# A fused long-convolution and MLP block on one core: integer table arguments, a buffer of their own for the small ones, and another order of the operations

## The chip, the cores and the metric

The kernel runs on one core of one Trainium2 chip. The metric is device time in microseconds. The kernel before takes 191.58 us (median of three runs, 191.40 to 192.06).

## What is computed

The input `x` has 2048 rows of 640. It is normalised (`xn`). Branch A makes `kv` from `k` (four taps of a short convolution) times `v`, convolves it causally with a filter of length 2048 per channel, and multiplies by `xn`. Branch B is an MLP with 1728 hidden units. The output joins them:

```python
xn = _layernorm(x)
kv = k_shift * v                        # k_shift: 4 taps, shift_k
y  = irfft(rfft(kv, 2*S) * rfft(ssm_k, 2*S))[:S] + kv * ssm_D
s  = xn * y
g  = silu(gelu(xn @ w1 + b1) @ w2 + b2)
return x + s * g
```

## The kernel before

**The transform by matmuls.** The two Fourier transforms are done in two steps of matmuls each. Step 1 uses a table `W` (128 x 16 x 128, bf16) of sines: for the filter (`K1_0` to `K1_15`, tile by tile, with `K1r_Q` for the last 128 channels of four tiles) and for `kv` (`U1_i`, `U1r_Q`). The casts that evict their PSUM banks are `Ke_i`, `Ker_Q`, `Ue_i`, `Uer_Q` (L175). A staged group of four tiles lies in half of the tile `st` and goes to DRAM in one 1.31 MB write, `Ks_Q` to `scrK` and `Us_Q` to `scrU` (L357). It comes back in another layout by eight loads each, `KL_s` (L528) and `UL_s` (L530), a load waiting for all four writes of its tensor. Step 2 (`K2`, `U2`, L544; `X2`, L559) uses the small table `F2`, followed by casts `Kf`, `Uf`; the products `pr`, `pq` (L571) and the first inverse step `i1`, `i1r` (L587, L615) with the small table `I1`; casts `ie`, `ir`; a write `cs_s` to `scrC` (L627), eight loads `cl_r` (L635), and the last step `i2_i` (L643) with the transposed `W` (`G`, from `gt0`, `gt1`).

**The MLP.** `f1` (L423) multiplies by `w1` in blocks of 128 hidden units, one chunk of 512 rows at a time (chunk 0 is partly cut into halves of 256); `ge` is its gelu on ACT (L427). `f2_i_h` (L463) multiplies tile `i` by half `h` of `w2` in 14 matmuls; `si` (L470) is the SiLU, `gx` (L473) the product with `xn`. A `/N` in the order cuts a matmul into two of 64 columns. `ym`, `ad`, `os` (L647, L651, L653) finish an output tile.

**Other parts.** `bn`, `rs`, `xn` are the layer norm (L370, L384, L391), `xt` and `xe` (L401, L404) the transposes of chunks 0 and 1, `xT2` and `xT3` (L409) those of chunks 2 and 3 by DMA. `kv0` to `kv4` (L502 to L511) are the short convolution on DVE: kv0 to kv2 cover four tiles each and take eight operations of 128 x 2560, kv3 and kv4 two tiles each and 128 x 1280. `U1_i` needs the kv of its tile: `U1_8` to `U1_11` need kv2, `U1_12` and `U1_13` kv3, `U1_14` and `U1_15` kv4. `wu0` to `wu5` (L321) are matmuls on zeros, `xl`, `Kl`, `kl`, `vl`, `w1l`, `w2l`, `skl` the loads of the inputs.

**The tables.** `grid` (L208, POOL) writes two ramps `tq` and `mq`, `fix` (DVE) shifts half of one. For three groups of tiles `wq0`, `wq1`, `wq2` (tiles 0 to 3, 4 to 9, 10 to 15) DVE makes the arguments: the product (L223), the same plus a quarter turn (L225), and an AND of each with 8191 (L226, L227). They lie as int32 in the still empty tile `w2`. `ws0` to `ws2` (L232, ACT) take two sines of each group. The small tables `F2` and `I1` get their arguments from `sm0` (POOL), `sm1` (DVE), `sm2` (POOL) and `sm3` (DVE, AND with 31), in the last quarter of `st`; `ss` (L277, ACT) takes their sines and `sx` (POOL) scales `I1`. The pool of staging slots lets the last quarter of `st` be used for other things only when all these operations are through (L325).

**What sets the order.** The program is a plan: each operation names its engine, what it reads and what it writes. A string `ORDER` lists all operations by hand; they are emitted in that order, so each engine's queue holds its own in that order, DMA queues included (SP for most transfers, POOL for a few). A name may carry the slots it takes (`@2.0`: PSUM banks or staging slots) and its engine (`/A`, `/D`, `/G`, `/S` for ACT, DVE, POOL, SP). Waits come from the buffers alone.

Of the kernel before, what the change touches and what calls it, by code (L numbers as in the profile page):

```python
# [110 lines left out]
def h3_block(ctx: ExitStack, tc: tile.TileContext, x_d, k_d, v_d, sk_d, K_d, D_d, w1_d, b1_d, w2_d, out_d):  # L111
    nc = tc.nc
    sb = ctx.enter_context(tc.tile_pool(name="sb", bufs=1))
# [104 lines left out]
    for g in range(len(TB) - 1):  # L218
        a, b = TB[g], TB[g + 1]

        def wq(e, a=a, b=b):
# [1 line left out]
            nc.vector.tensor_tensor(out=Pm[:, a:b, :], in0=tq[:, a:b, None].to_broadcast([P, n, 64]),  # L223
                                    in1=mq[:, None, :].to_broadcast([P, n, 64]), op=ALU.mult)
            nc.vector.tensor_single_scalar(out=Pc[:, a:b, :], in_=Pm[:, a:b, :], scalar=3 * L // 4, op=ALU.add)  # L225
            nc.vector.tensor_single_scalar(out=Pm[:, a:b, :], in_=Pm[:, a:b, :], scalar=L - 1, op=ALU.bitwise_and)  # L226
# [445 lines left out]
wu4@0 K1_15@2 Ke_15/A sm1 wq0 ws0 xl0 bn0 xl3 bn1 bn5 wu0@1 K1r_3@4 bn4 Ker_3/A id wu5@0 Kl2 sm2 sm3 b1c rs0 bn7 ss
rs1 K1r_1@6.2 gt1@1 K1_7@2 xn0 xn1 skl bn6 wu1@0 xt0@4.0 rs3 Ke_7/A xt1@5 K1_4@2 xe1/D xe0/A xl2 bn3 bn2 Ker_1/A w1l1
K1_6@4 Ke_6/A f1_0_0_2@0.0 xn4 Ke_4/A f1_0_0_4@6 w1l0 kl0 f1_0_0_1@7 xn6 xn5 xn7 f1_0_0_0@4 gte1/A xt4@5.1 xe4/A xt6@2
xt5@3 xe5/A ge_0_0_0 xt7@1 xe6/D f1_0_0_3@2 rs2 xn3 xt3@5 ge_0_0_4 xe7/D ge_0_0_3 f1_1_0_0@1.1 ge_1_0_0 w1l3
# [5 lines left out]
kv2_1a Ke_8/A Ks_2 f1_0_0_5@2 kv2_2m@0 kv2_2a kv2_3m@0 ge_0_0_5 f1_0_0_7@3 ge_0_0_7 U1_2@6.2 U1_3@4 Ue_3/A U1_0@0
Ue_0/A f1_1_0_3@2 kv2_3a kv2_4 ge_1_0_3 Kl1 Ue_2/A f1_1_0_10@3 ge_1_0_10 f1_1_0_4@4 w2l0 ge_1_0_4 f1_0_1_0@5 w2l1
U1r_0@0 Uer_0/A U1_1@6 Ue_1/A Us_0 f1_1_0_7@2 ge_1_0_7 ge_0_1_0 f1_1_0_9@3 ge_1_0_9 f1_0_0_10@4 ge_0_0_10 K1_2@0.0 kl3
kv3_0@0 K1_1@6 K1_3@2 kv3_1m@1 kv3_1a Ke_3/A f1_0_0_9@5 Ke_2/A ge_0_0_9 kv3_2m@1 f1_0_0_11@4 ge_0_0_11 kv3_2a Ke_1/A
Da f1_0_1_4@2 ge_0_1_4 f1_1_0_11@3 ge_1_0_11 K1r_0@0 Ker_0/A K1_0@4 kv3_3m@1 Ke_0/A U1_4@6.2 Ue_4/A f1_0_1_1@2 kv3_3a
# [5 lines left out]
Kf_2_1/A f2_3_0@4.0 Kf_0_0/A f2_3_1 si_3 bn11 bn8 gt0@6 KL3/G@2 K2_3_0@0 gte0/A Kf_3_0/D rs5 xn15 rs4 gx_2 K2_3_1@2  # L691
Kf_3_1/A K2_2_0@4 Kf_2_0/A f2_1_0@6.1 xn12 KL7@5 xn8 K2_7_0@0 Kf_7_0/A xn9 UL0@6 X2_0@2 xn13 xn14 Uf_0_2/D Kf_0_2/D
U2_0_0@4 Uf_0_0/A UL1@3 xn11 f2_1_1 si_1 U2_1_1@0 U2_1_0@4 Uf_1_0/A K2_7_1@2 Kf_7_1/A U2_0_1@6 gx_3 xn10 Uf_1_1/D gx_1
Uf_0_1/A UL2@8 f2_0_0@4.0 U2_2_1@0 Uf_2_1/A pr_1_0@0 X2_1@2 Kf_1_2/A pr_1_1@1 pr_0_0@2 Uf_1_2/A KL4/G@9 K2_4_0@6
Kf_4_0/A pr_0_1@3 f2_0_1 xT3@1 si_0 i1_1@0.2 ie_1_1/D ie_1_0/A X2_2@6 Kf_2_2/D f1_3_0_6@4.1 ge_3_0_6 f1_3_0_3@5
# [60 lines left out]
```

## Time and profile before

| | |
|---|---|
| median of three runs | 191.58 us |
| the profiled execution | 192.54 us |
| its span | 190.8 us |
| mean granted clock of PE | 0.978 |
| busy: DVE / ACT / POOL | 153.9 / 138.7 / 30.0 us |
| HBM read, written | 31.95 MB, 18.35 MB |

The span is the profiled execution from its first to its last instruction; 1.74 us of the 192.54 lie around it. PE is the matrix engine, PEld its loading of weights, DVE, ACT and POOL the vector, scalar and GpSimd engines, SP the one that issues most DMAs; "SPq" is the issue of a DMA by SP's queue. In the lines of the timeline, the first number is the start and the second the duration in microseconds; what stands in brackets is the idle time before an instruction and who ended it. In the rows by window come, behind the window, its length and the busy time of each engine with its number of instructions.

### The profile page before, as it was taken

The page shows a single profiled execution, that of the slowest core. Times are in us where ns is not written, and L with a number is a line of the kernel's source. Part 1 is how long each engine was busy: PE and PEld are TensorE (multiplying, and loading weights), DVE is VectorE, ACT ScalarE, POOL GpSimd, SP SyncE. Part 2 cuts the span into 40 slices and gives each one's busy share as a digit, 9 for nine tenths or more (in the row PEclk, how much of TensorE's full clock was granted, in tenths as well). Part 3 has the DMA queues.
Part 4 walks back from the last instruction along what each step waited for, and adds up shares of the span by engine and source line. Part 5 has one row for each costly group of instructions (what it writes and reads, how often), then busy time and mean ns, then how long its engine had stood idle before and what let it go on. Part 6 is the DMA issues. An engine that isn't in the chain of part 4 may idle for free.

```text
span 190.8 us, 5537 instructions
## 1 busy us (share of the span) xinstructions
PE 176.1 (92%) x2377; PEld 103.8 (54%) x2377; DVE 153.9 (81%) x241; ACT 138.7 (73%) x194; POOL 30.0 (16%) x61
## 2 busy tenths in 40 slices
PE   7889999999889874999979999999999999999991
PEld 2338564443456532566646444545454567679991
DVE  7999999999999891397995869799698511789983
ACT  5999999999979773457779889899969884111210
POOL 5745000070002100006200132101001103000000
PEclk9999999999999996699999999999999999999998
DMA  5999999999999999078999669930803469965283
GB/s 176 368 389 435 407 415 338 381 318 363 412 428 365 304 373 407 13 255 259 382 257 211 168 175 368 309 121 2 277 5 141 176 237 322 411 272 172 72 306 106
DMA packets 21530, 51.96 MB, mean 272 GB/s; under 512 B 6657, under 2 KB 14722, under 8 KB 20098
## 3 DMA queue, kind: packets, MB, share of 16 engines
q1 hardware_dynamic: 18912, 40.47, 61.0%
q0 software_dynamic: 2448, 11.14, 16.2%
q8 instruction: 18, 0.29, 0.7%
q14 instruction: 6, 0.05, 0.1%
q10 hardware_dynamic: 146, 0.00, 0.0%
HBM read 31.95 MB, written 18.35 MB: 264 GB/s over the span
## 4 chain that ended last, share of the span: by engine, by line
PE 44%; DVE 31%; DMA 20%; issue 2%; ACT 1%; SPq 1%; POOL 0%; POOLq 0%; DVEq 0%
PE ps L423 15%; PE ps L463 15%; DVE lat L506 8%; DVE lat L509 8%; DMA k<-scrK 6%; DMA lat<-scrU 6%; PE ps L587 4%; DMA lat<-scrC 4%; DVE stats L370 3%; PE ps L544 3%; DMA scrU<-st 3%; DVE lat L502 3%; DVE v L511 2%; PE ps L643 2%; DVE xn L391 1%
## 5 line engine op out<-in xcount | busy, mean ns | idle before, releaser
L463 PE MATMUL ps<-w,hT 128*128 128x320 bf16 (+2 forms) x588 | 66.8, 303 | 3.3 <-ACT st L175 1.3
L423 PE MATMUL ps<-xnT,w 128*128 128x512 bf16 (+3 forms) x325 | 61.0, 362 | 0.0
L463 PEld LDWEIGHTS <-hT 128*128 128x128 bf16 (+2 forms) x588 | 48.0, 105 | 20.2 <-issue 6.9
L423 PEld LDWEIGHTS <-w 128*128 128x128 bf16 (+1 forms) x325 | 26.8, 101 | 28.4 <-issue 4.8
L175 ACT CAST st<-ps 128x1024 bf16<-128x1024 f32 x39 | 38.2, 1041 | 2.4 <-DMA scrU<-st 1.2
L427 ACT ACTIVATE hT<-ps,b1f 128x512 bf16<-128x512 f32 (+1 forms) x57 | 35.2, 679 | 3.7 <-PE ps L423 3.4
L470 ACT ACTIVATE sl<-ps 128x640 bf16<-128x640 f32 (+1 forms) x17 | 11.5, 675 | 31.8 <-PE ps L463 30.3
L175 ACT CAST k<-ps 128x1024 bf16<-128x1024 f32 (+2 forms) x25 | 18.8, 775 | 4.3 <-PE ps L544 3.7
L473 DVE TENSOR_TENSOR xn<-xn,sl 128x640 bf16<-128x640 bf16 (+1 forms) x17 | 7.9, 463 | 16.3 <-ACT sl L470 16.3
L175 DVE CAST k<-ps 128x1024 bf16<-128x1024 f32 (+2 forms) x12 | 12.1, 1022 | 10.1 <-ACT hT L427 2.4
L506 DVE TENSOR_TENSOR lat<-k,lat 128x2560 bf16<-128x2560 bf16 (+1 forms) x15 | 19.4, 1294 | 0.3
L509 DVE TENSOR_TENSOR lat<-lat 128x2560 bf16<-128x2560 bf16 (+1 forms) x15 | 18.4, 1226 | 0.5
L175 ACT CAST v<-ps 128x1024 bf16<-128x1024 f32 (+2 forms) x20 | 16.7, 858 | 2.1 <-PE ps L615 1.2
L647 DVE TENSOR_TENSOR xn<-ps,xn 128x640 bf16<-128x640 f32 x16 | 12.8, 817 | 2.4 <-PE ps L643 2.4
L370 DVE BATCH_NORM_STATS2 stats<-x 128x6 f32<-128x320 bf16 x32 | 13.6, 468 | 0.0
L544 PEld LDWEIGHTS <-F 64*32 64x32 bf16 x512 | 6.0, 92 | 8.9 <-DMA k<-scrK 3.9
L175 DVE CAST lat<-ps 128x1024 bf16<-128x1024 f32 (+2 forms) x9 | 8.2, 921 | 1.5 <-PE ps L587 0.9
L321 PE MATMUL ps<-hT 128*128 128x512 bf16 x24 | 7.7, 465 | 1.2 <-DVE hT L206 1.2
L587 PE MATMUL ps<-st,I 32*64 32x512 bf16 x256 | 8.6, 380 | 0.0
L544 PE MATMUL ps<-k,F 64*32 64x256 bf16 x224 | 5.1, 291 | 3.6 <-DMA k<-scrK 3.6
L175 ACT CAST lat<-ps 128x1024 bf16<-128x1024 f32 (+2 forms) x8 | 6.3, 804 | 1.9 <-PE ps L544 1.6
L511 DVE TENSOR_TENSOR v<-lat,v 128x2560 bf16<-128x2560 bf16 (+1 forms) x5 | 6.1, 1225 | 0.5 <-DMA v<-in_v 0.4
(99 smaller groups left out, 181.4 us busy)
## 6 DMA issues: line engine op xcount, KB each, us to landing
...
```

What stands on the lines that cost most here:

```text
L175: (nc.scalar.copy if e == "ACT" else nc.vector.tensor_copy)(out=out_, in_=in_)
L370: nc.vector.bn_stats(out=stats[:, i, h, :], in_=x_t[:, i, h * H:(h + 1) * H])
L423: nc.tensor.matmul(out=pb.v[us, 0:b - a], lhsT=w1_t[:, ft, t, us], rhs=xnTb[c].v[:, a // P:b // P, t, :], start=(t == 0), stop=(t == DT - 1))
L427: nc.scalar.activation(out=hTb[c].v[:, ft, a:b], in_=pb.v[:, 0:b - a], func=ACT.Gelu_apprx_tanh, bias=b1_f[:, ft:ft + 1], scale=1.0)
L463: nc.tensor.matmul(out=pb.v[us, h, 0:H], lhsT=hTb[c].v[0:M, ft, q * P + us.start:q * P + us.stop], rhs=w2_t[0:M, ft, hs], start=(ft == 0), ...
L470: op("si_" + nm, "ACT", lambda e, hs=hs, n=n: nc.scalar.activation(out=s_.v[:, hs].rearrange("p (h c) -> p h c", c=H), in_=pb.v[:, n[0]:n[ ...
L506: op("kv%d_%dm" % (r, j), "DVE", lambda e, i=i, n=n, j=j, t=t, wb=wb: nc.vector.tensor_tensor(out=t.v[:, 0:n, :], in0=k_t[:, i + 3 - j:i + ...
L509: op("kv%d_%da" % (r, j), "DVE", lambda e, n=n, t=t, a=a: nc.vector.tensor_tensor(out=a.v[:, 0:n, :], in0=a.v[:, 0:n, :], in1=t.v[:, 0:n, ...
L511: op("kv%d_4" % r, "DVE", lambda e, i=i, n=n, a=a: nc.vector.tensor_tensor(out=v_t[:, i:i + n, :], in0=a.v[:, 0:n, :], in1=v_t[:, i:i + n, ...
L544: nc.tensor.matmul(out=pb.v[32 * j:32 * j + 32, a, ri * wd:(ri + 1) * wd], lhsT=F2_t[64 * a:64 * a + 64, ri, :], rhs=B.v[64 * a:64 * a + 6 ...
L587: nc.tensor.matmul(out=pb[j // 2].v[64 * a:64 * a + 64, j % 2, :], lhsT=I1_t[32 * j:32 * j + 32, m, :], rhs=o[w][32 * j:32 * j + 32, a, r, ...
L647: op("ym_%d" % i, "DVE", lambda e, i=i, pb=pb: nc.vector.tensor_tensor(out=xn_t[:, i, :], in0=pb.v.rearrange("p a b -> p (a b)")[:, 0:D], ...
```

## The change

There are three parts. First, `tq` and `mq` are int32 ramps, and `wq` is cut in two: `wm` makes the product and the quarter turn, on DVE or on POOL, and `wq` does both ANDs in one DVE operation over both halves. In the new order `wm1` is on POOL, `wm0` and `wm2` on DVE. Second, the arguments of the small tables (`fiq`) get a tile `fi` of their own, with a buffer `fqb`; the last quarter of `st` no longer waits for `sm3` and `ss`. Third, `ORDER` is new throughout. The number of warm-up operations stays six. There are 19 operations with `/N` (18 before): five of `f1` and 14 of `f2` (eight and ten before).

```diff
-    tq, mq = scr[:, 0:NT], scr[:, 16:80]
+    tq, mq = scr[:, 0:NT].bitcast(I32), scr[:, 16:80].bitcast(I32)
...
-    fiq = scr[:, 384:640].bitcast(I32)
+    fi_t = sb.tile([P, 256], F32, name="fi")
+    fiq = fi_t[:].bitcast(I32)
...
+        def wm(e, a=a, b=b):
+            n, en = b - a, nc.gpsimd if e == "POOL" else nc.vector
+            en.tensor_tensor(out=Pm[:, a:b, :], in0=tq[:, a:b, None].to_broadcast([P, n, 64]),
+                             in1=mq[:, None, :].to_broadcast([P, n, 64]), op=ALU.mult)
+            en.tensor_single_scalar(out=Pc[:, a:b, :], in_=Pm[:, a:b, :], scalar=3 * L // 4, op=ALU.add)
+
         def wq(e, a=a, b=b):
-            n = b - a
-            nc.vector.tensor_tensor(out=Pm[:, a:b, :], in0=tq[:, a:b, None].to_broadcast([P, n, 64]),
-                                    in1=mq[:, None, :].to_broadcast([P, n, 64]), op=ALU.mult)
-            nc.vector.tensor_single_scalar(out=Pc[:, a:b, :], in_=Pm[:, a:b, :], scalar=3 * L // 4, op=ALU.add)
-            nc.vector.tensor_single_scalar(out=Pm[:, a:b, :], in_=Pm[:, a:b, :], scalar=L - 1, op=ALU.bitwise_and)
-            nc.vector.tensor_single_scalar(out=Pc[:, a:b, :], in_=Pc[:, a:b, :], scalar=L - 1, op=ALU.bitwise_and)
+            v = Pq.rearrange("p (i a b) -> p i a b", i=2, a=NT)[:, :, a:b, :]
+            nc.vector.tensor_single_scalar(out=v, in_=v, scalar=L - 1, op=ALU.bitwise_and)
...
-        op("wq%d" % g, "DVE", wq, reads=[tmb], writes=[Pqb[g]])
+        op("wm%d" % g, "DVE|POOL", wm, reads=[tmb], writes=[Pqb[g]])
+        op("wq%d" % g, "DVE", wq, reads=[], writes=[Pqb[g]])
...
-    op("sm2", "POOL", sm2, writes=[smb])
+    op("sm2", "POOL", sm2, writes=[smb, fqb])
...
-    op("ss", "ACT", ssin, reads=[smb, cb], writes=[Fb, Ib])
+    op("ss", "ACT", ssin, reads=[fqb, cb], writes=[Fb, Ib])
```

Two stretches of the order that the steps below speak of. At the start, before and after:

```diff
-grid zz wu3@0 fix c0 Kl4 wq2 b1l sm0 Dl wu2@1 ws2 wq1 ws1 one1 K1_12@2.0 xl1 Ke_12/A K1_14@4 Ke_14/A K1_13@6 Ke_13/A
+xl3 zz c0 wu4@0 grid fix sm0 wu0@1 Kl4 xl2 wm2 wm0 wq0 ws0 wq2 sm1 wu2@2 ws2 K1_13@4.0 Kl2 wm1/G wu5@3 wq1 bn4 bn5 bn6
```

Around the first reading back of K, before and after (some names at the ends are cut off):

```diff
-U1_6@2 Ue_6/A Us_1 U1r_2@6.0 f2_2_0 U1_11@4 Uer_2/A kv4_0@1 kv4_1m@0 kv4_1a U1_9@2 Ue_11/A si_2 kv4_2m@0 kv4_2a U1_8@6
-Ue_8/A Ue_9/A f2_5_1@4.0 kv4_3m@0 kv4_3a f2_5_0 U1_12@0.2 kv4_4 si_5 gx_5 U1_13@6 Ue_13/A U1_10@2 KL1@0 KL2@1 Ue_12/A
-bn10 f2_6_1@4.0 K2_1_0@6 Ue_10/A Kf_1_0/A K2_1_1@0 Kf_1_1/A f2_6_0 Us_2 si_6 gx_6 U1_15@2 Ue_15/D bn9 U1r_3@6 U1_14@0
-sx f2_4_1@4.0 Uer_3/A Ue_14/A Us_3 f2_4_0 bn12 bn13 KL0/G@4 K2_0_1@6 K2_0_0@2 bn14 bn15 si_4 gx_4 Kf_0_1/A K2_2_1@0
+Ue_4/A si_7 gx_7 U1r_2@4 kv3_3m@1 kv3_3a kv3_4 kv4_1m@1 Uer_2/A kv4_0@0 kv4_1a Ue_8/A U1_11@0 kv4_2m@1 kv4_2a KL1@0
+KL2@1 kv4_3m@1 kv4_3a kv4_4 KL0@4 f2_6_0@2.0 U1_10@4 U1_9@6 f2_6_1 Ue_11/A Ue_9/A bn14 U1_6@0 Ue_10/A Us_2 ss U1r_1@6
+Ue_6/A Uer_1/A si_6 gx_6 f2_2_0@4.1 K2_1_0@0 xl4 Us_1 Kf_1_0/A K2_1_1@6 Kf_1_1/A f2_2_1 si_2 gx_2 U1_12@2.0 Ue_12/D
+U1_14@0 Ue_14/A bn11 U1r_3@6 Uer_3/A bn8 U1_15@4 bn10 f2_4_0@0.0 Ue_15/A U1_13@6 Ue_13/A Us_3 bn12 KL3/G@2 K2_3_1@2
```

More of the change, by code (lines that the diff above doesn't have):

```diff
@@ L186, in h3_block @@
     Wb = [Buf() for _ in range(len(TB) - 1)]
-    Fb, Ib, idb, b1b, b1rb, Db, cb, tmb, smb = (Buf() for _ in range(9))
+    Fb, Ib, idb, b1b, b1rb, Db, cb, tmb, smb, fqb = (Buf() for _ in range(10))
     Gb = [Buf() for _ in range(2)]
@@ L208, in grid @@
     def grid(e):
-        nc.gpsimd.iota(tq, pattern=[[1, NT]], base=0, channel_multiplier=32, allow_small_or_imprecise_dtypes=True)
-        nc.gpsimd.iota(mq, pattern=[[2, 64]], base=1, channel_multiplier=0, allow_small_or_imprecise_dtypes=True)
+        nc.gpsimd.iota(tq, pattern=[[1, NT]], base=0, channel_multiplier=32)
+        nc.gpsimd.iota(mq, pattern=[[2, 64]], base=1, channel_multiplier=0)
     op("grid", "POOL", grid, writes=[tmb])
     op("id", "POOL", lambda e: make_identity(nc, ident[:]), writes=[idb])
-    op("fix", "DVE", lambda e: nc.vector.tensor_single_scalar(out=tq[64:P, :], in_=tq[64:P, :], scalar=16.0 - 2048.0, op=ALU.add),
+    op("fix", "DVE", lambda e: nc.vector.tensor_single_scalar(out=tq[64:P, :], in_=tq[64:P, :], scalar=16 - 2048, op=ALU.add),
        reads=[], writes=[tmb])
@@ L272, in h3_block @@
     op("sm1", "DVE", sm1, writes=[smb])
-    op("sm2", "POOL", sm2, writes=[smb])
-    op("sm3", "DVE", lambda e: nc.vector.tensor_single_scalar(out=fiq, in_=fiq, scalar=31, op=ALU.bitwise_and), writes=[smb])
+    op("sm2", "POOL", sm2, writes=[smb, fqb])
+    op("sm3", "DVE", lambda e: nc.vector.tensor_single_scalar(out=fiq, in_=fiq, scalar=31, op=ALU.bitwise_and), writes=[fqb])
     def ssin(e):
@@ L670 @@
 ORDER = """
-grid zz wu3@0 fix c0 Kl4 wq2 b1l sm0 Dl wu2@1 ws2 wq1 ws1 one1 K1_12@2.0 xl1 Ke_12/A K1_14@4 Ke_14/A K1_13@6 Ke_13/A
[L672 to L675, printed above, removed]
@@ L681 @@
[L681 to L685, printed above, removed]
@@ L691 @@
[L691 to L695, printed above, removed]
@@ L716 @@
-ym_9 ad_9 os_9 f2_12_1/N@2.1 f2_12_0/N si_12 gx_12 ad_12 os_12 f2_15_0/N si_15_0 gx_15_0 os_15_1 ad_15_0 os_15_0
+xl3 zz c0 wu4@0 grid fix sm0 wu0@1 Kl4 xl2 wm2 wm0 wq0 ws0 wq2 sm1 wu2@2 ws2 K1_13@4.0 Kl2 wm1/G wu5@3 wq1 bn4 bn5 bn6
+b1l Ke_13/A sm2 ws1 one0 bn7 id wu3@6 bn3 skl K1r_3@0 Ker_3/A K1_15@2 wu1@7 K1_14@4 Ke_15/A sm3 Ke_14/A bn2 K1_12@0
+K1_5@6.2 K1r_1@2 Dl rs3 xl1 bn1 Kl0 w1l3 xl0 xn6 xn7 xt6@4.0 xn5 Ke_12/A Ke_5/A Ker_1/A K1_6@0 gt0@5 xt7@6 kl0 rs2 xn4
+xn2 xe7/D xt5@7 xe6/A xt4@2 xe4/A xe5/D rs1 xn1 xt2@3.1 Ke_6/A gt1@4 f1_1_0_9@6.0 b1c gte1/A xe2/D K1_7@2 w1l1 w1l2
@@ new lines @@
+K1_4@0 f1_1_0_11@7 Ke_4/A kv0_0@0 w1l0 ge_1_0_9 f1_1_0_10@4 ge_1_0_10 Kl3 gte0/A f1_1_0_8@0 Ks_3 xn3 xt3@1 f1_1_0_12@6
+ge_1_0_12 bn0 rs0 kv0_1m@1 kv0_1a xt1@4 ge_1_0_11 vl0 xe1/A f1_1_0_0@5 ge_1_0_0 xn0 xt0@6 f1_1_0_2@7 ge_1_0_8 xe3/D
+Ke_7/A xe0/D f1_0_0_8@1.1 kv0_2m@1 kv0_2a ge_0_0_8 K1r_2@4.0 Ker_2/A f1_1_0_1@6 kl1 kv0_3m@1 f1_0_1_2@0 kv0_3a kv0_4
+ge_0_1_2 ge_1_0_2 K1_8@2 Ke_8/A f1_0_0_1@1 kl2 ge_0_0_1 kv1_1m@1 kv1_0@0 kv1_1a one1 f1_0_1_0@4 xl5 bn15 ge_1_0_1
+f1_1_0_5@5 ge_1_0_5 bn13 K1_9@2 kv1_2m@1 kv1_2a Ke_9/A ge_0_1_0 Kl1 kv1_3m@1 kv1_3a K1_10@0 Ke_10/A Ks_1 f1h_1@7 geh_1
@@ new lines @@
+f1_0_0_2/N@6 f1h_0@5 f1_1_0_6/N@2 K1_11@0 Ke_11/A f1_0_0_5@3 f1_0_0_4@4 vl1 f1_0_0_10@7 ge_1_0_6 kv1_4 ge_0_0_5
+ge_0_0_2 geh_0 Da Ks_2 ge_0_0_4 K1_3@0.2 K1_1@2 Ke_1/A Ke_3/A f1_0_0_0@6 ge_0_0_0 f1_0_0_3@5 ge_0_0_3 f1_1_0_3@4
+K1_2@2 Ke_2/A ge_0_0_10 K1_0@0 Ke_0/A f1_1_0_7@6 ge_1_0_7 f1_0_0_7@5 ge_0_0_7 f1_0_1_3@2 ge_0_1_3 U1_0@0.0 w2l1
+ge_1_0_3 K1r_0@6 Ker_0/A f1_0_0_9@3 ge_0_0_9 f1_1_0_4@5 Ue_0/A f1_0_0_11@2 ge_0_0_11 kv2_1m@1 kv2_0@0 kv2_1a vl2
+kv2_2m@1 kv2_2a kv2_3m@1 kv2_3a kv2_4 f1_0_1_4@4 ge_0_1_4 w2l0 Ks_0 U1r_0@6 U1_3@0 Ue_3/A f1_0_0_12@3 f1_0_1_1@2
@@ new lines @@
+Uer_0/A kl3 kv3_1m@1 U1_2@0 Ue_2/A ge_1_0_4 f1_0_0_6@4 ge_0_0_6 U1_5@6.2 ge_0_0_12 kv3_0@0 kv3_1a ge_0_1_1 U1_1@0
+f2_5_0@4.0 Ue_1/A Us_0 kv3_2m@1 kv3_2a Ue_5/A f2_5_1 si_5 vl3 gx_5 f2_7_0@2.1 U1_4@0 U1_8@6.0 U1_7@4 Ue_7/A f2_7_1
+Ue_4/A si_7 gx_7 U1r_2@4 kv3_3m@1 kv3_3a kv3_4 kv4_1m@1 Uer_2/A kv4_0@0 kv4_1a Ue_8/A U1_11@0 kv4_2m@1 kv4_2a KL1@0
+KL2@1 kv4_3m@1 kv4_3a kv4_4 KL0@4 f2_6_0@2.0 U1_10@4 U1_9@6 f2_6_1 Ue_11/A Ue_9/A bn14 U1_6@0 Ue_10/A Us_2 ss U1r_1@6
+Ue_6/A Uer_1/A si_6 gx_6 f2_2_0@4.1 K2_1_0@0 xl4 Us_1 Kf_1_0/A K2_1_1@6 Kf_1_1/A f2_2_1 si_2 gx_2 U1_12@2.0 Ue_12/D
@@ new lines @@
+U1_14@0 Ue_14/A bn11 U1r_3@6 Uer_3/A bn8 U1_15@4 bn10 f2_4_0@0.0 Ue_15/A U1_13@6 Ue_13/A Us_3 bn12 KL3/G@2 K2_3_1@2
+f2_4_1 Kf_3_1/A K2_2_0@4 Kf_2_0/A si_4 K2_3_0@6 gx_4 f2_1_1@2.1 f2_1_0 si_1 rs5 bn9 rs4 xn13 xn15 Kf_3_0/A K2_0_1@4
+K2_2_1@0 Kf_2_1/A sx xn14 f2_3_1@2.0 Kf_0_1/D K2_0_0@4 KL4@6 K2_4_1@6 K2_4_0@0 Kf_0_0/A Kf_4_0/A xn12 f2_3_0 si_3
+UL1@5 U2_1_1@4 Kf_4_1/D X2_1@6 xn11 gx_1 Uf_1_1/A U2_1_0@0 UL0/G@3 Uf_1_0/A xn9 xT3@0 f2_0_0@2.1 Uf_1_2/D Kf_1_2/D
+pq_1_0@2 pq_1_1 U2_0_1@4 Uf_0_1/A xn8 X2_0@6 U2_0_0@0 Uf_0_0/A Kf_0_2/A pr_1_1@3 pr_1_0@0 xn10 Uf_0_2/A pq_0_0 f2_0_1
@@ new lines @@
+xT2@1 si_0 i1_1@4.0 ie_1_1/A pr_0_1@1 ie_1_0/D pr_0_0@0 UL2/G@8 gx_3 f1_3_0_1@6.0 ge_3_0_1 f1_3_0_7@7 ge_3_0_7
+f1_3_0_4@2 ge_3_0_4 X2_2@0 Kf_2_2/D U2_2_0@4 Uf_2_0/A U2_2_1@6 Uf_2_1/A Uf_2_2/D pr_2_1@3 f1_3_0_9@3 ge_3_0_9 i1_0@4.0
+ie_0_0/D ie_0_1/A f1_3_0_12@2 ge_3_0_12 pq_2_1@0 UL3/G@9 X2_3@6 U2_3_0@0 Uf_3_2/A Uf_3_0/A f1_3_0_8@3 f1_2_0_2@2.1
+pq_0_1 ge_3_0_8 pq_2_0 UL4@10 ge_2_0_2 i1r_0@4.0 pr_2_0@1 ir_1_0/A f1_2_0_4@3 ir_0_0/A ir_0_1/A ir_1_1/A ge_2_0_4
+Kf_3_2/D U2_3_1@6 UL6@7 U2_6_0@4 Uf_6_0/A U2_4_0@0 Uf_4_0/A Uf_3_1/D pr_3_0@2 f1_2_0_10@2 KL5@0 ge_2_0_10 i1_2@6.4
@@ new lines @@
+ge_2_0_3 ge_2_0_12 X2_7@4 Uf_7_2/D Kf_7_2/D K2_7_1@6 U2_7_1@2 Uf_7_1/A f1h_2@1 geh_2 Kf_7_1/D pq_7_1 f1_2_0_9/N@0
+ge_2_0_9 i1_6@4.2 f1_3_0_5@1 ie_6_0/A ie_6_1/D ge_3_0_5 pq_7_0 U2_5_1@6 Uf_5_1/D K2_7_0@4 Kf_7_0/A pr_4_1@0 K2_5_1@2
+Kf_5_1/A cs_1 f1_3_0_3@0 ge_3_0_3 i1r_3@6.4 ir_6_1/A f1_3_0_0@1 ir_7_1/A ir_7_0/D ge_3_0_0 f1_2_0_7@2 pq_4_0 i1r_2@4.0
+ir_6_0/D cs_6/S ge_2_0_7 pr_7_0@2 ir_4_1/A ir_5_1/A ir_5_0/A f1_3_0_11@3 ir_4_0/A ge_3_0_11 pr_4_0@1 i1_4@6.0 ie_4_0/A
+pr_7_1@3 i1_7@4.2 ie_7_1/A ie_4_1/D ie_7_0/A f2_8_0@6.0 cs_2/S cs_4/S f1_3_0_10@0 pr_5_0@0 pr_5_1@1 i1_5@2.4 ie_5_1/D
```

41 lines of the change are left out of this document (14 added, 27 removed).

## The prediction

> **What bounds the kernel now.** I read the page's engine line and slices first.
>
> ```profile
> span 190.8 us, 5537 instructions
> ...
> PE 176.1 (92%) x2377; PEld 103.8 (54%) x2377; DVE 153.9 (81%) x241; ACT 138.7 (73%) x194; POOL 30.0 (16%) x61
> ...
> PEclk9999999999999996699999999999999999999998
> DMA  5999999999999999078999669930803469965283
> ```
>
> PE is busy for 92% of the span. Its only weak place inside the kernel is slices 15 and 16 (72 to 81 us), where its clock also falls. Up to there the DMA engines are full. The table of windows, cut around that place, has per row the busy time of PE, PEld, DVE, ACT and POOL, then clock, DMA share and GB/s:
>
> ```profile
> 40.00:50.00 10.00, 10.00 (x66) 4.62 (x66) 9.86 (x7) 10.00 (x16) 2.34 (x2) 1.00 0.99 346
> ...
> 60.00:70.00 10.00, 9.29 (x71) 5.78 (x68) 9.31 (x13) 7.90 (x11) 1.81 (x2) 1.00 0.97 338
> 70.00:75.00 5.00, 1.42 (x36) 0.60 (x35) 2.31 (x6) 1.35 (x3) 0.00 (x0) 0.81 1.06 392
> 75.00:80.00 5.00, 5.00 (x26) 2.47 (x26) 0.39 (x1) 2.41 (x4) 0.00 (x0) 0.51 0.28 117
> 80.00:85.00 5.00, 4.99 (x80) 3.43 (x79) 4.90 (x13) 2.70 (x4) 0.00 (x0) 1.00 0.51 197
> ...
> 95.00:100.00 5.00, 3.77 (x82) 2.25 (x79) 4.87 (x8) 3.44 (x4) 0.00 (x0) 1.00 1.10 262
> ```
>
> Before 60 us PE, DVE, ACT and DMA are all full, so no one of them can be relieved alone. At 70 us PE starves. The timeline and the chain say why:
>
> ```profile
> 61.11 0.33 SPq L357 DMA_DIRECT2D scrU<-st  x1
> ...
> 61.55 1.56 SPq L528 DMA_DIRECT2D k<-scrK  x2
> ...
> 71.01 11.13 SPq L357 DMA_DIRECT2D scrU<-st  x2
> ...
> 73.93 0.58 PEld L544 LDWEIGHTS <-F 64*32 64x32 bf16 x32 [3.91 <-DMA k<-scrK]
> ...
> 74.92 3.92 PE L463 MATMUL ps<-w,hT 128*128 128x320 bf16 x14
> ```
> ```profile
> 61.55 12.34 DMA k<-scrK
> ...
> 81.81 5.50 DMA scrU<-st
> ...
> 88.42 11.57 DMA lat<-scrU
> ```
>
> KL1 and KL2 (L528, the read-back of the transformed K) are issued on SP right behind the write Us_1 and land 12 us later. PE waits 3.6 us for them, the clock drops to half, and the next fourteen L463 matmuls take 3.92 us where 2.0 is usual. By the clock column half speed lasts (0.19×5 + 0.49×5)/0.5 = 6.8 us, about 3.0 us of work lost. So this place costs 3.6 + 3.0 = 6.6 us, and it delays the last writes of U (Us_3, issued 81.81) and the U reads, after which PE is short of work again (95 to 100 us). From 100 us on PE is nearly full to the end.
>
> The Trainium skill ("TensorE: Matmul & The Clock Gate", Part 1) puts the drop to half clock after one idle window of about 3.4 us, and the return after as much steady work. The trace agrees: 3.6 us idle, then half clock.
>
> **How I price the new order.** For each engine I add up what is listed ahead of a point, each operation at its start-to-start time in rows of this trace: f2 half tile 1.9, f1 1.09, i1 1.0, a K1/U1/K2/U2 piece 0.22 on PE; cast 0.96, 512-wide gelu 0.62 on ACT; kv step 1.42 or 0.75, bn 1.0 on DVE. Clock time less this sum is the engine's **lag**. Before: PE's lag is 5.1 at its first f1 (14.5 us), 6.1 at U1_0, 8.8 at U1_8, 13.5 at K2_1_0, 16.6 at f2_4_1 (80.06 us, sum 63.5) and 23.4 at its last matmul (186.9, sum 163.5). ACT's is 3.4 at its first gelu and 5.0 at Ue_6 (61.1); DVE's is 0.9 at kv0_0, 3.6 at kv2_4, 5.2 at kv4_4 (70.9). PE's whole sum is 163.4 after: no matmul work goes. What can change is the lag, above all the 16.6.
>
> **The change part by part.**
>
> *Tables.*
>
> ```profile
> 1.51 0.56 DVE L223 TENSOR_TENSOR w<-st 128x384 int32<-128x384 f32 x1
> ...
> 2.11 0.36 DVE L225 TENSOR_SCALAR w<-w 128x384 int32<-128x384 int32 x1
> ...
> 6.37 0.29 DVE L226 TENSOR_SCALAR w<-w 128x256 int32<-128x256 int32 x1
> ...
> 8.36 0.87 POOL L268 TENSOR_TENSOR st<-st 128x64 f32<-128x64 f32 x3
> ...
> 9.29 0.35 POOL L269 CAST st<-st 128x192 int32<-128x192 f32 x1
> ```
>
> Before, wq2, wq1, wq0 hold DVE 1.99 + 1.70 + 1.27 = 4.96 us. After, DVE keeps two product-and-add pairs (0.56+0.36, 0.41+0.29) and three ANDs of double length. A 768-element AND lies between 0.57 (0.36 plus the slope from 0.29 to 0.36) and 0.72 (two of 0.36); I take 0.70, and 0.50 for 512. Sum 3.5 us: 1.4 saved. POOL's pair of 384 elements is not in the trace. From below it is two casts (0.70 us), from above the 64-element rows scaled by six (0.29×6 + 0.46×6 = 4.5); nearest in size is the cast of 192, doubled for each: 1.4 us. POOL is free at 2.2, so wm1 is done at 3.6, and DVE wants it at 5.0: hidden. At 4.5 us DVE would wait 1.7 us with bn4 to bn7 and all kv behind. sm2, `id` and rs3 queue behind wm1 on POOL; rs3 ends near 12.4, before DVE wants xn6 at 13.1.
>
> ACT starts worse: ws0 at 3.7 (before ws2 at 3.18), then ws2 to 6.1; K1_13 waits for it and for Kl4, now second in the DMA queue (6.0), so the first cast starts 6.6 instead of 6.05, and ws1 comes after it. Following casts and slots to the first gelu (ge_1_0_9, 20.75, sum 15.9) gives lag 4.85: ACT is 1.4 us worse.
>
> *Own buffer.* It frees the last quarter of `st` from sm3 and ss, so ss moves from 11.4 us to behind Ue_10. It costs ACT its 0.7 us either way, but F2 and I1 now exist only when ss is through. The instruction lists show five table loads after, seven before, and none around the late sine. The row of a load is 1.28 us and work resumes 1.30 us after it starts (18.66 to 19.96). The Trainium skill ("ScalarE: Activation LUTs", What ACT_TABLE_LOAD costs) charges about 2.7 us for a switch; the trace shows 1.3, and by the list there is none here.
>
> *The order up to K2.* DVE's sum to kv4_4 is 66.8 (65.8 before): 1.4 us saved, bn13 and bn15 pulled ahead, small shifts. kv0_0 waits for kl0 (5.57 MB queued through it, 5.24 before, landed 16.4: now 17.6); lag 2.5 there and 5.5 to 6.8 at kv4_4: 72.3 to 73.6, about 2 us later than before. SP's queue: KL1 lands with 22.77 MB against 24.74 plus 1.31 on POOL's; the rate to 73.6 us is 0.373 MB/us. Us_1 and xl4 now stand behind KL1. Us_0 goes when Ue_1 is cast, ACT sum 51.0 + lag 4.0 to 6: 55 to 57; KL1 follows it and vl3 and lands 65.5 to 67.5. ACT, lag 1.4 worse: Ue_10 59.9 + 6.4 = 66.3, ss 67.0, Ue_6 67.9. K2_1_0 takes Ue_6's bank, so it starts at **68.2** (before 73.94), with F2 and KL1 there. Then U1_14 at kv4_4 (73), U1_15 at si_2's bank, f2_4_0 at 74.5 behind Ue_14's bank, sum 63.8: lag 10.7. PE idles in pieces of at most 1.5 us, so no half clock. Us_3 is issued about 77.6 (before 81.81).
>
> *Behind it.* The U reads follow Us_3 by 5.6 us as before: UL1 lands 87, U2_1_1 is reached at 89. DVE has 14.6 us of work against PE's 11.8 between rs5 and pr_1_0, ending 95.2 when PE is at i1_1 at 94.6: 0.6 us. xT3 lands near 95, wanted 95.6. The last scrC loads have 13.2 us of PE work over them after i1_5 (before 10.7), needing 9. So I give the rest the growth it had before, 23.4 − 16.6 = 6.8.
>
> **Sum.** PE ends 163.4 + 10.7 + 6.8 + 0.6 = 181.5; store and end 3.9 as before: span 185.4, against 190.8. The profiled execution was 192.54 for its span; the median of the runs, 191.58, is 0.8 above the span. So **186.2 us**, 5.4 less (2.8%).
>
> **Rivals.**
> - *More*: with the U reads earlier, the 1.7 us of idle PE between 90 and 100 us go too, and the tail waits: 183 to 184. For it: the tail cover above. Against: DVE is full in that stage.
> - *Given back*: wm1 at its upper bound, or kv4_4 2 us later, or i1_1 and xT3 late by 2 to 4 us: 188.5 to 191. The parts where two things meet within 1 us (xT3, pr_1_0, kl0) speak for it. That the integer tables do nothing is in here: DVE +1.4 us moves kv4_4 and U1_14, giving 187.6.
> - *Slower*: K2_1_0 is still starved. KL1 waited for behind Us_0 needs 10 to 12 us from issue before; if Us_0 slips to 60, KL1 lands at 72. A gap of 2.7 us or more brings the half clock (in this trace it fell 2.7 us into the gap) with 3.0 to 3.4 us: 5.9 lost, all of the gain. A gap of 4 us gives 193. It decides at KL1 landing about 71 us.
>
> Chances: forecast (184 to 188.5) 0.45, more 0.14, given back 0.13, no change 0.05, slower 0.23. Changes under 0.3% can't be told apart here. Faster 0.72, same 0.05, slower 0.23. The range 182.5 to 192.5 leaves out about 0.05 below and 0.15 above.
>
> **What would show it.** PE clock 1.0 through 65 to 85 us; K2_1_0 at 67 to 70; Us_3 issued 76 to 79; five table loads; POOL's pair 1 to 2 us; lag at f2_4_0 near 10.7. I am wrong if PE has one gap of over 2.7 us, if kv4_4 ends after 75, or if lag grows by more than 8 us behind f2_4_0.

## The result and the profile after

The changed kernel takes **202.18 us** (median of 4 runs, 200.85 to 203.77), the kernel before 191.82 us (4 runs, 191.40 to 193.78): ratio 1.052, 95% interval 1.042 to 1.063. It is slower; the forecast was 186.2 us with a range up to 192.5. The profiled execution took 200.85 us for a span of 199.0 us. The time of the kernel before goes with the clock that a run was granted (over 53 runs beside the experiments: median 189.6 us at 0.995 or more, 191.3 at 0.985 to 0.995, 192.6 below), and its profiled execution, at 0.978, is one of the last kind.

The page's head, its engine line, and three of the rows by slice of the changed kernel (a slice is 5 us):

```profile
span 199.0 us, 5631 instructions
...
PE 177.2 (89%) x2427; PEld 108.0 (54%) x2427; DVE 152.4 (77%) x236; ACT 136.9 (69%) x192; POOL 31.8 (16%) x62
...
PE   7669999999989996999219999999999999999990
...
PEclk9997999999999999999955999999999999999999
DMA  6999999599949999689799845870707759964056
```

The hole of the kernel before at 72 to 81 us is gone. A new one, two slices wide, is at 95 to 104 us, with half clock behind it, and a dip of the clock is in the fourth slice (15 to 20 us). PE's busy time is the same within 1.1 us; the span is 8.2 longer. The windows, with the columns as before:

```profile
60.00:70.00 10.00, 9.76 (x82) 5.68 (x81) 9.22 (x14) 7.96 (x11) 0.00 (x0) 1.00 1.01 331
70.00:75.00 5.00, 5.00 (x72) 3.12 (x68) 4.83 (x8) 4.74 (x7) 0.00 (x0) 1.00 1.05 399
75.00:80.00 5.00, 3.42 (x46) 2.00 (x42) 4.01 (x11) 3.42 (x5) 0.00 (x0) 1.00 0.86 358
...
90.00:95.00 5.00, 5.00 (x126) 3.44 (x108) 4.11 (x8) 4.37 (x5) 0.57 (x1) 1.00 1.25 210
95.00:100.00 5.00, 0.86 (x37) 0.43 (x35) 3.26 (x5) 1.09 (x2) 0.00 (x0) 0.96 0.88 130
100.00:105.00 5.00, 1.06 (x32) 0.54 (x33) 0.00 (x0) 0.17 (x1) 0.00 (x0) 0.50 1.19 157
105.00:110.00 5.00, 5.00 (x46) 2.35 (x44) 1.56 (x2) 2.53 (x4) 0.00 (x0) 0.51 1.36 175
```

From 70 to 75 us PE is full where it had been starved. From 95 to 105 it does 1.92 us of work in 10, DVE and ACT stop too, and up to 110 us the DMA engines are busy (share 0.88 to 1.36) while they move only 130 to 175 GB/s, less than half of the 399 that they reached at 70 us. The timeline of that place:

```profile
88.19 0.87 POOL L534 DMA_DIRECT2D k<-scrU  x1
...
88.77 19.16 SPq L413 DMA_TRANSPOSE xnT<-xn  x2
89.06 1.51 POOL L534 DMA_DIRECT2D lat<-scrU  x2
...
95.64 0.22 PE L563 MATMUL ps<-k,F 64*32 64x128 bf16 x2
...
103.94 0.41 PE L563 MATMUL ps<-k,F 64*32 64x128 bf16 x14 [8.08 <-issue]
104.04 0.73 PE L548 MATMUL ps<-k,F 64*32 64x256 bf16 x16
104.70 3.92 PE L467 MATMUL ps<-w,hT 128*128 128x320 bf16 x14
```

SP issues the transposes xT3 and xT2 (L413) from 88.77 us on, and POOL issues the reads UL0, UL2 and UL3 (L534) within the same microsecond. By the records of DMA packets the last packet of xT3 ends at 107.1 us, 18.3 after its issue (8.1 before). By the profile's landings UL2 and UL3 take 15.9 and 17.0 us from issue (11.6 and 5.4 before). PE stops in the middle of one operation, X2_0 (L563), after 18 of its 32 matmuls, so no operand can be what it waits for; the profile names no releaser ("issue"). Then the next fourteen L467 matmuls take 3.92 us in place of 2.0.

PE's lag (clock time less the work listed ahead, as in the prediction) through the changed kernel: 7.5 us at K1_4 (19.4 us), 11.6 at K2_1_0 (72.16), 13.7 at f2_4_0 (77.54), 14.9 at U2_1_0 (92.89), 23.4 at U2_0_0 (104.04, behind the stop), 26.4 at f1_3_0_7 (111.25), 30.0 at its last f2. At U2_1_0 the changed kernel is 2.7 us *ahead* of the kernel before (92.89 against 95.62). All of the loss comes between 93 and 111 us, and a little at the very end.

### The profile page after: what moved, and what is told of

Its sections match the earlier page's. It is cut to its first block, busy times and chain, and to the rows that moved or that the text cites. A ratio compares the mean times of both kernels' runs of the same rounds, so it can differ in the third digit from the quotient of the medians.

```text
span 199.0 us, 5631 instructions
## 1 busy us (share of the span) xinstructions
PE 177.2 (89%) x2427; PEld 108.0 (54%) x2427; DVE 152.4 (77%) x236; ACT 136.9 (69%) x192; POOL 31.8 (16%) x62
## 4 chain that ended last, share of the span: by engine, by line
PE 68%; ACT 15%; issue 5%; POOL 4%; DMA 3%; DVE 3%; ACTq 0%; POOLq 0%; DVEq 0%
PE ps L467 28%; PE ps L427 23%; ACT st L176 8%; PE ps L548 4%; ACT hT L431 4%; PE ps L591 4%; DMA scrU<-st 3%; PE ps L647 2%; PE ps L405 2%; PE ps L563 1%; PE ps L342 1%; PE ps L619 1%; POOL rstd L389 1%; ACT hT L447 1%; DVE w L224 1%
## 5 line engine op out<-in xcount | busy, mean ns | idle before, releaser
L467 PE MATMUL ps<-w,hT 128*64 128x320 bf16 (+3 forms) x658 | 67.1, 303 | 3.4 <-ACT st L176 1.6
L467 PEld LDWEIGHTS <-hT 128*64 128x64 bf16 (+3 forms) x658 | 51.1, 106 | 17.1 <-issue 7.2
L474 ACT ACTIVATE sl<-ps 128x640 bf16<-128x640 f32 (+1 forms) x17 | 11.4, 674 | 28.6 <-PE ps L467 28.6
L176 ACT CAST k<-ps 128x1024 bf16<-128x1024 f32 (+2 forms) x26 | 21.3, 849 | 12.3 <-PE ps L548 9.5
L374 DVE BATCH_NORM_STATS2 stats<-x 128x6 f32<-128x320 bf16 x32 | 13.7, 469 | 0.8 <-DMA x<-in_x 0.8
L176 DVE CAST v<-ps 128x1024 bf16<-128x1024 f32 (+2 forms) x10 | 9.8, 982 | 5.3 <-PE ps L548 2.4
L176 ACT CAST v<-ps 128x1024 bf16<-128x1024 f32 (+2 forms) x13 | 10.2, 804 | 1.9 <-PE ps L591 1.0
L176 ACT CAST lat<-ps 128x1024 bf16<-128x1024 f32 (+2 forms) x14 | 10.5, 777 | 0.8 <-PE ps L591 0.8
L176 DVE CAST k<-ps 128x512 bf16<-128x512 f32 (+2 forms) x10 | 8.6, 872 | 3.2 <-PE ps L591 1.8
L575 DVE TENSOR_TENSOR st<-k,v 128x512 bf16<-128x512 bf16 (+1 forms) x4 | 3.2, 821 | 8.6 <-ACT k L176 8.6
L563 PE MATMUL ps<-k,F 64*32 64x128 bf16 x128 | 2.4, 227 | 8.1 <-issue 8.1
L176 DVE CAST lat<-ps 128x1024 bf16<-128x1024 f32 (+2 forms) x7 | 6.4, 918 | 3.5 <-ACT hT L431 1.6
(99 smaller groups left out, 192.5 us busy)
```

The lines of the kernel that those rows point to most:

```text
L176: (nc.scalar.copy if e == "ACT" else nc.vector.tensor_copy)(out=out_, in_=in_)
L374: nc.vector.bn_stats(out=stats[:, i, h, :], in_=x_t[:, i, h * H:(h + 1) * H])
L467: nc.tensor.matmul(out=pb.v[us, h, 0:H], lhsT=hTb[c].v[0:M, ft, q * P + us.start:q * P + us.stop], rhs=w2_t[0:M, ft, hs], start=(ft == 0), ...
L474: op("si_" + nm, "ACT", lambda e, hs=hs, n=n: nc.scalar.activation(out=s_.v[:, hs].rearrange("p (h c) -> p h c", c=H), in_=pb.v[:, n[0]:n[ ...
```

## The experiments

The theory: reads on POOL's queue and transposes on SP's, in flight together, slow each other, and PE's stop follows. Its rivals: PE's own instructions come late whatever the DMAs do; reads on POOL's queue are slow by themselves; or the integer tables cost the time. Ratios are to runs of the kernel before on the same chip.

### Two reads behind the transposes

```diff
-... pr_0_0@0 UL2/G@8 gx_3 ...
+... pr_0_0@0 UL2@8 gx_3 ...
-... pq_2_1@0 UL3/G@9 X2_3@6 ...
+... pq_2_1@0 UL3@9 X2_3@6 ...
```

> The changed kernel with one edit: the U reads UL2 and UL3 go out on SP's queue, behind the two chunk transposes xT3 and xT2, instead of on POOL's queue beside them. Theory 1 (the transposes by DMA and the POOL queue's reads slow each other from 93 to 106 us, and PE's own instruction fetch is stuck in that traffic): PE's stop of 8.1 us in X2_0 goes and the half clock behind it too, 8.1 + 3.4 = 11.5 us; span 186 to 189, xT3 and xT2 done by 101. Rival (PE waits for the data of UL0, or the stop has nothing to do with that traffic): a stop of 5 us or more stays between 93 and 110 us, span 196 to 200.

Measured: 194.75 us (4 runs), ratio 1.022 [1.013, 1.032]; span 192.4. Of the 8.2 us of span between the two kernels, 6.6 came back; by the ratios it is 3.0 of 5.2%. The span stays over the 186 to 189 us of the theory. The transposes' packets flow from 92.5 to 102.8 us (92.0 to 110.8 in the changed kernel), the stop in X2_0 is 1.14 us, and there is no half clock behind it. The chain shows what took its place:

```profile
96.01 1.14 issue
...
101.64 5.11 DMA lat<-scrU
```

UL2 now waits on SP's queue behind xT2 and X2_2 waits for it, 2.5 us. The collision is the main cause; putting the reads behind the transposes pays part of it back.

### Sixty more PE instructions ahead

```diff
-f1_1_0_9@6.0  f1_1_0_11@7  f1_1_0_10@4  f1_1_0_8@0  f1_1_0_12@6  f1_0_0_8@1.1
+f1_1_0_9/N@6.0  f1_1_0_11/N@7  f1_1_0_10/N@4  f1_1_0_8/N@0  f1_1_0_12/N@6  f1_0_0_8/N@1.1
```

Of the six operations five are of chunk 1 and one is of chunk 0.

> The changed kernel with six early f1 operations of chunk 1 and one of chunk 0 cut into 64-column halves (/N), at the same matmul time: 60 more PE instructions ahead of the stop, nothing else moved. Theory 1 (PE runs out of fetched instructions): PE stops after the same number of instructions, 1728 and a few, so some 60 instructions earlier in the work: in U2_0_1 or at the end of f2_0_0 instead of inside X2_0, for 6 to 9 us; span 197 to 201. Rival (PE waits for data there): it stops in X2_0 after 18 of its 32 matmuls as now.

Measured: 202.08 us (one run), span 200.3. The stop did not stay at its instruction number: X2_0, U2_0_0, f2_0 and i1_1 now ran without a stop, and PE stood still later, 11.4 us long. The chain of waits of this kernel, and its PE line:

```profile
87.91 21.80 DMA xnT<-xn
109.71 0.05 issue
109.76 2.32 PE ps L427 x5
```
```profile
97.33 1.07 PE L591 MATMUL ps<-st,I 32*64 32x512 bf16 x32
109.76 2.74 PE L427 MATMUL ps<-xnT,w 128*128 128x512 bf16 x6 [11.36 <-DMA xnT<-xn]
```

This time the releaser is named: f1_3_0_1, the first operation that reads xT3, waits for the transpose. Neither of the two forecasts came: PE passed its recorded instruction 1728 at 94.4 us without a stop, and the last fetch of instructions ahead of it (more on these at the end) ran from 89.46 to 90.40 us, before the first packets of the transposes (91.18). So the stop in X2_0 was not needed for the loss. With it or without it, PE can't pass f1_3_0_1 before xT3 has landed.

### The integer tables in the old order

The kernel before with `wm`, `wq` and the buffer `fqb` as changed, and its own `ORDER`, into which only the new operations are put:

```diff
-... c0 Kl4 wq2 b1l sm0 Dl wu2@1 ws2 wq1 ws1 ...
+... c0 Kl4 wm2 wq2 b1l sm0 Dl wu2@1 ws2 wm1/G wq1 ws1 ...
-... sm1 wq0 ws0 ...
+... sm1 wm0 wq0 ws0 ...
```

> The integer tables with wm1 on POOL and the buffer of their own, in the order of before. Theory 1 (the loss is in the new order, behind 90 us): span 188.5 to 191.5, a little below before, because DVE does 1.4 us less. Rival (the integer tables or POOL's product cost the time, from the start on): span over 193, with PE's first f1 later than 16 us.

Measured: 192.22 us (4 runs), ratio 1.011 [1.001, 1.021]; profiled span 188.5. The transposes flow from 94.7 to 102.2 us, with reads beside them only up to 96.4. Tables and buffer bring nothing in the old order, by the interval they cost 0.1 to 2.1%; they aren't what cost 5%.

### The collision put into the kernel before

```diff
-... Uf_0_1/A UL2@8 ...
+... Uf_0_1/A UL2/G@8 ...
-... UL3@10 ...
+... UL3/G@10 ...
```

> The kernel before with one edit, the opposite of the first: UL2 and UL3 on POOL's queue beside the transposes. Theory 1: xT3 and xT2 together take over 10 us (7.3 in before), and PE has a stop of over 3 us between 93 and 112 us; span 194 to 200. Rival (the collision is not what matters): span within 1.5 us of before's 190.8.

Measured: 194.82 us (193.92 and 195.72), ratio 1.022 [1.009, 1.036]. The transposes take 9.4 us (98.6 to 108.0) in place of 7.4. PE's line there:

```profile
105.67 0.29 PE L559 MATMUL ps<-k,F 64*32 64x128 bf16 x10 [1.83 <-issue]
...
106.27 3.98 PE L423 MATMUL ps<-xnT,w 128*128 128x512 bf16 x10 [0.20 <-DMA xnT<-xn]
```

PE stops for 1.83 us inside X2_2, again with no releaser, then waits 0.2 us for xnT, and a half clock of 3.4 us follows (106.2 to 109.6). Two more reads on POOL's queue are enough to cost some 3.5 us there (1.8 and 0.2 of standing, half of 3.4). The direction is the theory's; the sizes are below it (over 10 us and over 3 us were expected).

### Three reads ahead of the transposes

```diff
-U2_1_0@0 UL0/G@3 Uf_1_0/A xn9 xT3@0   ... UL2/G@8 ...   ... UL3/G@9 ...
+U2_1_0@0 UL0@3 UL2@8 UL3@9 Uf_1_0/A xn9 xT3@0
```

> The changed kernel with the reads UL0, UL2 and UL3 issued by SP ahead of the first transpose (xT3), in place of GpSimd's queue beside and behind it. Theory (reads that flow beside the transposes slow them, and PE's stop follows): the four reads take about 1.8 us each and end near 96 us, the transposes flow alone from there and take 7 to 8 us as before (7.4) and as with the integer tables alone (7.5), against 18.8 in the changed kernel; the stop of 8.08 us shrinks to below 1.5, the 2.5 us wait for lat<-scrU that was left with the reads behind the transposes goes too, and the time is 189 to 192 us. Rival 1 (PE's own instruction fetch is late at instruction 1728, whatever the reads do): a stop of over 4 us stays there, 196 to 200 us. Rival 2 (it is the place in line: behind four reads the transposes start 4 us later and are as late): PE waits 2 to 4 us for xnT instead, 193 to 196 us.

Measured: 192.77 us (4 runs), 0.8 over the range of the theory, ratio 1.013 [1.003, 1.022], span 190.7. On one queue the three reads follow each other at 1.7 to 1.8 us and are through at 95.7 us but for a few late packets (up to 97.2); the transposes flow behind them, from 95.3 to 103.0. PE waits 1.1 us in X2_0 and 0.9 for xnT, none for `lat`. 8.3 us of span are gone. What this left over is in the tail (below).

### The early half clock

```diff
-NWARM = 6
+NWARM = 8
-... xn6 xn7 xt6@4.0 ...
+... xn6 xn7 wu6@4 wu7@5 xt6@4.0 ...
```

> The changed kernel with two more warm-ups (8 matmuls of 128x512 on zeros) in PE's idle time ahead of the transpose xt6, 11.9 to 13.7 us. Theory on the early loss: the half clock from 14.3 to 17.7 us, 1.7 us of lag, comes from that idle time; with the warm-ups the clock stays at 1.0 and the lag at K1_4 falls from 7.5 to about 6. What is gained there is worth up to 1.7 us at the end if everything behind moves with it: 199 to 202 us, the stop near 95 us still 8 us or more. Rival: the early loss is VectorE's, which works 1.93 of every 2 us up to 14 us: the lag at K1_4 stays over 7 and the time at 202.

> Both of these edits together: the reads ahead of the transposes and the two warm-ups. If they are two separate losses, the time is that of the reads ahead of the transposes less 1 to 1.7 us, 187.5 to 191 us, and so no slower than the kernel before (191.6). If transposes that land late set the end, the second edit adds nothing to the first.

Measured: 205.33 us (ratio 1.079 [1.062, 1.097]) with the changed kernel's reads, 193.86 us (ratio 1.020 [1.009, 1.030]) with the reads ahead. Both misses. The half clock near 14 us did go and PE came earlier, but PE gained nothing by it. PE's waits in the first of the two:

```profile
PE ps L427 <- DMA xnT<-xn: 9.0, 1, 9.0
PE ps L563 <- issue: 2.1, 1, 2.1
```

What was won at the start is waited away at f1_3_0_1, and the transposes took still longer (91.8 to 112.9 us). With the reads ahead PE waited 2.0 us for xnT, then had a half clock of 3.4 us at 100.7. Why the transposes took 21 us here and not 19 isn't shown.

### Stores in the tail

SP's queue of the changed kernel at the end:

```profile
186.77 0.33 SPq L657 DMA_DIRECT2D out<-x  x1
189.08 0.33 SPq L666 DMA_DIRECT2D out<-x  x1
189.46 4.37 SPq L657 DMA_DIRECT2D out<-x  x6
193.93 0.39 SPq L666 DMA_DIRECT2D out<-x  x1
194.37 0.94 SPq L657 DMA_DIRECT2D out<-x  x2
195.40 1.38 SPq L666 DMA_DIRECT2D out<-x  x3
```

From 189.08 us on SP issues thirteen more stores without a pause; one of them takes 1.92 us to issue (at 190.43), the others 0.33 to 0.45. Five of them (os_0, os_8, os_3, os_7, os_6) were ready at 178.4 to 183.2 us and stood behind os_2 (186.77), which waits for ad_2. The last addition ends at 194.78, the last store is issued at 196.39: 1.6 us late (0.03 before). The edit, on top of the reads ahead:

```diff
-... ym_7 i2_2@4 ad_7 ad_6            ... ad_10 os_0 os_10 os_11 os_6 os_3 ad_5 ...  si_12 os_8 os_7
+... ym_7 i2_2@4 ad_7 os_0 os_8 os_3 os_7 ad_6 os_6   ... ad_10 os_10 os_11 ad_5 ...  si_12
```

> The kernel with the reads ahead of the transposes, and in the tail five stores of finished rows (os_0, os_8, os_3, os_7, os_6) moved on SP's queue ahead of the store os_2, behind which they waited although their rows were done at 169.8 to 174.5 us. Theory (the end is SP's line of stores: from os_13 on it issues one per 0.4 to 0.5 us without a pause and reaches os_15_1 at 187.77 us, 1.66 us behind the last addition at 186.11): the last store issues at about 186.2, and 1.6 us go: 191.2 us, 190.5 to 191.8, level with the kernel before. Rival (the stores' transfers, not their issue, end last): under 0.5 us, 192.3 or more.

> The same with UL3 on SP at its old place, behind the second transpose, so that only UL0 and UL2 stand ahead of the first. UL3 took 1.8 us ahead of xT3, so xT3 starts and lands 1.8 us sooner, near 97.5 us: PE's 0.9 us wait for xnT goes. X2_3 and U2_3_0, which read UL3, come near 109 us, and UL3 lands near 103: no new wait. 0.5 to 1.5 us under the kernel with three reads ahead. Rival (PE has no wait of note left there, what is left is its own work): the same time within 0.3 us.

> The changed kernel with the five stores moved alone, the reads as it has them. Theory: two separate losses, so the tail gives 1.6 us here too: 200.6 us (199.5 to 201.7), PE's stop near 95 us still 8 us. Rival (the transfers end last): no change, 202.2 us.

Measured: 190.99 us (12 runs), ratio 1.002 [0.999, 1.006], with the stores moved, 1.8 us under the kernel with the three reads ahead; no store takes over 0.45 us to issue now. With UL3 behind the transposes: 190.71 us (12 runs), ratio 0.998 [0.993, 1.003]; no wait for xnT is left. Its 0.3 us under the other can't be told from nothing. With the stores alone: 201.78 us (4 runs), ratio 1.055 [1.046, 1.063]. That one is inconclusive: the changed kernel itself spreads over 2.9 us, and in the profiled execution here the transposes took still longer (92.5 to 115.3 us), so that PE stood 7.9 us in X2_0 and then 5.2 us for xnT.

> The best so far (UL0 and UL2 ahead of the first transpose, UL3 behind the second, the five stores moved) with the two warm-ups ahead of xt6. Theory: the half clock of 3.4 us near 14 us costs about 1.0 us at K2_1_0 (72.2 with it, 71.2 without), and PE no longer waits for xnT or a read behind it, so what is gained at the start reaches the end this time: 189.8 to 190.5 us, 0.3 to 0.9 under 190.7 (some of whose runs were without that half clock), and about 0.5% under the kernel before. Rival (the transposes land as late as they did and PE waits for xnT again, as it did 2.0 us with three reads ahead and the warm-ups): 190.7 to 192 us.

Measured: 191.63 us (6 runs), ratio 1.011 [1.003, 1.018]. A miss; the warm-ups help in none of three places. A new PE stop of the "issue" kind, 1.41 us, came at 109.7 us.

### The transposes behind the reads, the reads left on POOL

```diff
-U2_1_0@0 UL0/G@3 Uf_1_0/A xn9 xT3@0 f2_0_0@2.1 ...
+U2_1_0@0 UL0/G@3 Uf_1_0/A xn9 f2_0_0@2.1 ...
-xT2@1 si_0 ...
+xT2@1 xT3@0 si_0 ...
```

> The changed kernel with the first transpose (xT3) moved behind the second (xT2) on SP's queue. xT2 waits for xn10, which VectorE writes at 97.8 us, so both transposes come behind the three reads on GpSimd's queue in time; the reads stay on that queue. Theory (it is the overlap of transposes and reads, not the queue that the reads are on): UL2 and UL3 take about 2 us each in place of 11 and 16 from issue, the transposes take 7 to 8.5 us alone, from about 99.5 to 107 us, PE's stop of 8.08 us at 95.6 shrinks below 1.6 us, and in its place PE waits 4 to 6 us for xnT, since xT3 now comes last; f1_3_0_7 starts at 106.5 to 108 (111.25), the time is 197 to 200 us. Rival 1 (reads on GpSimd's queue are slow in themselves): UL3 still takes over 10 us. Rival 2 (PE's late instructions do not depend on the transposes): a stop of 6 us or more stays at instruction 1728.

Measured: 198.89 us (4 runs), ratio 1.032 [1.022, 1.043]; span 196.9. It came as the theory has it, with PE's wait and f1_3_0_7 (108.68) 0.7 us over their bounds: the three reads on POOL's queue landed 5.3, 7.1 and 8.0 us after issue (6.0, 15.9 and 17.0 in the changed kernel), the transposes took 6.4 us (99.6 to 106.0), the stop in X2_0 shrank to 0.5, and PE waited 6.7 us for xT3, which now comes last. Its chain:

```profile
95.90 0.47 issue
...
101.50 5.02 DMA xnT<-xn
106.52 0.05 issue
106.57 5.21 PE ps L427 x15
```

So it is neither POOL's queue nor PE's instructions by themselves. It is transposes and reads in flight together. The row of L413 gives the same answer in one number, the time that SP needs to issue a transpose (min, median, max in ns): the changed kernel, then the three reads ahead, then this one:

```profile
L413 SPq DMA_TRANSPOSE xnT<-xn x2: 7544/9531/11518, 88.8 to 100.4; - x2
```
```profile
L413 SPq DMA_TRANSPOSE xnT<-xn x2: 3604/6118/8632, 89.3 to 98.3; - x2
```
```profile
L413 SPq DMA_TRANSPOSE xnT<-xn x2: 3117/3138/3160, 98.3 to 101.5; - x2
```

## Why the prediction was wrong, step by step

**Tables: right in effect, wrong in size.** The rows of the changed kernel:

```profile
L230 DVE TENSOR_SCALAR w<-w x3: 427/550/852, 3.9 to 5.6; 128x768 int32<-128x768 int32 x2, 128x512 int32<-128x512 int32 x1
L224 DVE TENSOR_TENSOR w<-st x2: 559/800/1041, 1.5 to 2.3; 128x384 int32<-128x384 int32 x1, 128x256 int32<-128x256 int32 x1
...
L224 POOL TENSOR_TENSOR w<-st x1: 934/934/934, 2.2 to 2.2; 128x384 int32<-128x384 int32 x1
L226 POOL TENSOR_SCALAR w<-w x1: 1515/1515/1515, 3.2 to 3.2; 128x384 int32<-128x384 int32 x1
```

POOL's pair took 0.93 + 1.51 = 2.45 us (I took 1.4, bounds 0.70 to 4.5) and ended at 4.71, ahead of wq1 at 5.59: hidden, as forecast. DVE has 4.27 us in place of 4.96: 0.7 saved, not 1.4. wm0's product of 256 elements, which begins while POOL's product runs, took 1.04 us (0.41 in the kernel before); wq2 took 0.85 where wq1, of the same shape, took 0.55.

**Own buffer: right.** Five table loads, none around the late sine.

**The order up to K2: right in kind, 3 to 4 us short.** K2_1_0 starts without a gap, and from 65 to 85 us the clock is 1.0 and PE is full but for one wait of 1.55 us (up to 77.54, for Ue_14's bank). But it starts at 72.16, not 68.2. I took its start from ACT's chain and KL1's landing (67.9; forecast 65.5 to 67.5) and never checked it against PE's own line: 60.6 us of work ahead, the lag of 7.5 measured at 19.4 us, and the 3.7 that the lag had grown in the kernel before up to U1_8 give 71.8. Part of the 7.5 is the start: PE waits 1.84 us for xn behind POOL's `rs3`, and the half clock of 3.4 us that follows costs 0.5 to 1 us (K2_1_0 at 72.2 to 72.3 in the six executions of the new order with it, 71.2 to 71.7 in the five without). All that comes behind is then late by 3.0 to 3.6 us: f2_4_0 77.54 (74.5), Us_3 81.00 (77.6), UL1 landed 90.6 (87), U2_1_1 92.39 (89).

**Behind it: the step that failed.** "xT3 lands near 95, wanted 95.6. [...] So I give the rest the growth it had before." xT3 landed at 107.1. Behind f2_4_0 the lag grew by 16.3 us, not 7.4: two of the prediction's own signs of being wrong (one gap of over 2.7 us, growth over 8 us). I had dated xT3 by its issue and a flow of about 7 us, and counted the three U reads that the new order moves from SP's queue to POOL's as transfers without an effect on what SP's queue carries. In the kernel before SP's queue itself had kept them apart: UL2 ahead of xT3, UL3 behind xT2, one after the other (two reads of K on POOL's queue overlapped xT3 there, by 1.6 us). The rival "given back" named xT3, but priced it at 2 to 4 us late; it was 12, by a mechanism that no rival names. From f1_3_0_7 to the end the lag grew 3.6 us, as it had before (3.7 behind i1_1).

**The half clock: the threshold does not hold.** The prediction let a gap of 2.7 us or more bring the half clock, from one gap. In the later runs it came behind gaps of 1.83 us (the collision in the kernel before) and 2.04 us (reads ahead, with warm-ups), and it did not come behind 2.09 us (the tables alone) and 2.54 us (two reads behind). The length of the gap alone does not decide it. Behind the gap it lasted 6.0 us of work in the kernel before (73.94 to 79.90) and 5.9 in the changed one (103.94 to 109.85).

**Tail: half right.** PE did cover the scrC loads, but "store and end 3.9 as before" became 5.4, by the line of stores on SP.

**The base.** I added 0.8 us to the span, the median of the runs less the span of another execution; every run's time is 1.7 to 1.9 us above its own span. That is 1.0 us. And the 3.0 us of half clock that I let the new order save belong to the profiled execution: the kernel before ran in 188.2 to 191.3 us whenever its clock was 0.995 or more.

**The sum.** Forecast span 185.4; + 3.0 (order up to f2_4_0) + 8.9 (behind it) + 1.5 (tail) = 198.8, measured 199.0. With both faults mended the new order takes 190.7 us, ratio 0.998: no version was shown to be faster than the kernel before.
